# The setup phase of an attention kernel in another order

## The chip, the core and the metric

The kernel runs on one core of a Trainium2 chip. A core has a matrix engine (TensorE, PE in the profile, with its weight loads as PEld), a vector engine (VectorE, DVE), an activation engine (ScalarE, ACT), GpSimd (POOL) and SyncE (SP), which here only issues transfers. Each engine works through its own queue of instructions in order and waits on semaphores for the others. The metric is the device time of one execution in microseconds (us). A profile is a record of one such execution, and its times count from the start of its span.

## What is computed

With S = 2048 rows, D = 640 columns, 32 heads of 20 columns and F = 1728:

```python
xn = layernorm(x)                                  # rows of 640, eps 1e-5
q, k, v = split(xn @ wqkv)                         # 32 heads of 20
p = softmax(q @ k.T * 20 ** -0.5)                  # 2048 x 2048 for each head
s = (p @ v) @ wo
g = silu((sigmoid(xn @ w_gate) * (xn @ w_up)) @ w_down)
out = x + s * g
```

x, the weights and the result are bf16.

## The kernel before

**Tiling.** The 2048 rows lie in 16 tiles of 128 rows. The scores of one head for 512 queries and 128 keys fill one PSUM bank of 128 x 512. Four heads make a group; 4 query chunks times 8 groups give 32 passes of 64 banks, 2048 banks in all. The exponential of a bank is taken either on ACT (L868, two or three banks at a time, tiles `sc`) or on DVE with five instructions (L879 to L896, one bank at a time, tile `spare`).

**The main loop** is planned while the program is built. A planner keeps clocks of PE, ACT and DVE and emits, for PE, the next scores, the next products with V (L962, `oacc`), or a piece of a background job (tiles `work`, two PSUM banks): the rest of K (`k_job`: five matmuls of 128 x 512, an eviction L425 and a maximum L112 on DVE), the rest of V (`v_job`: five matmuls of 128 x 320 and a copy L129 on DVE), the queries of the next passes (`q_job`), the gate, up and down products, and the output. A job has a pass by which it must be done: V for the first 16 heads is due in pass 0, and so is K of group 1, without which the scores of pass 1 can't be computed. If such work is late, the planner emits it without scores between (`must_fill`). The engines then run the emitted order, at whatever pace the chip has.

**The setup phase** before it loads x in seven transfers and three weight blocks, computes the layernorm, and makes the first pass's operands: the transposed normalised rows `xnT`, K and its bound for group 0, Q for the first 512 queries and group 0, and V for the first 16 heads in 8 row tiles (`V_SETUP`). Its steps are listed as operations with an engine, an estimated duration, predecessors and a rank, and a list scheduler takes the one that can start first by these estimates; that gives the order of each engine's queue. The steps of a row tile t:

- `ln_stats` (DVE, L197 twice and L198): mean and variance
- `ln_sqrt` (ACT, L201) and `ln_scale` (DVE, L207 reciprocal, L208 product -mean/std), for one or two tiles at once
- `ln_apply` (L212): x * rstd + nb, on GpSimd for tiles 0 to 13, on DVE for 14 and 15
- `transpose` (PE, L220, five matmuls into a PSUM tile `tp`, three of them in turn) and `xnT_evict` (ACT, L223)

For four row tiles follow `k_mm` (PE, L102, PSUM tile `ps_k`, two in turn), `k_max` (DVE, L112) and `k_add` (ACT, L231); when all four are done, `k_bound` (DVE, L108 and L109, tile `bound`), `q_bound` (PE, L250, added into the query's PSUM bank) and `q_evict` (ACT, L255), which gives `qT`. The first scores need `qT`. The eight V products (PE, L124, tile `ps_v`) and their copies (ACT, L240) stand between.

GpSimd first clears and fills small tiles (L172 to L183), then applies the layernorm, pads the weights (`pad_copy`, L191), and after the list clears and fills what the main loop needs (L302 to L315), among it `wo_pad` (L311) and `identf`, behind which SP's 32 loads of `wo_pad` wait.

Of the kernel before, what the change touches and what calls it, by code (L numbers as in the profile page):

```python
# [8 lines left out]
FP32 = mybir.dt.float32  # L9
BF16 = mybir.dt.bfloat16  # L10
ACT = mybir.ActivationFunctionType
ALU = mybir.AluOpType
AXISX = mybir.AxisListType.X

P = 128
HEAD = 32
GH = 4
# [18 lines left out]
def kernel(  # L36
# [11 lines left out]
    nc = tc.nc  # L48
# [3 lines left out]
    S, D = x2.shape  # L52
    Dh = D // HEAD
    KD = D // P
# [52 lines left out]
    def k_bound(g):  # L107
        nc.vector.tensor_reduce(out=mk[:, g:g + 1], in_=mk_all[:, g, :], axis=AXISX, op=ALU.max)  # L108
        nc.vector.tensor_scalar(out=bound[:, g, :], in0=esum, scalar1=mk[:, g:g + 1], scalar2=None, op0=ALU.mult)  # L109

    def k_max(src, g, c):
        nc.vector.tensor_reduce(out=mk_all[:, g, c:c + 1], in_=src, axis=AXISX, op=ALU.max,  # L112
                                apply_absolute_value=True)

    def q_abs(ps):
        absq = wk.tile([P, QC], BF16, tag="absq", bufs=1, name="absq")
        high = ps.bitcast(U16).rearrange("p (q two) -> p q two", two=2)[:, :, 1]
        nc.vector.tensor_scalar(out=absq.bitcast(U16), in0=high, scalar1=0x7FFF, scalar2=None,
                                op0=ALU.bitwise_and)
        return absq  # L120
# [7 lines left out]
    def v_copy(copy, ps, tt, h0, h1):  # L128
        copy(out=v_all[:, tt, h0:h1, 1:1 + Dh],  # L129
             in_=ps[:, 0:(h1 - h0) * Dh].rearrange("p (h e) -> p h e", e=Dh))  # L130
# [8 lines left out]

    V_SETUP = 8
    qTs = {}
    with tc.tile_pool(name="setup", bufs=1) as sp, \
            tc.tile_pool(name="ps0", bufs=1, space=bass.MemoryType.PSUM) as ps0:
# [3 lines left out]
        stats = sp.tile([P, TT, 2, nc.vector.BN_STATS_DIM], FP32, name="stats")  # L149
        mv = sp.tile([P, TT, 2], FP32, name="mv")  # L150
        rstd = sp.tile([P, TT], FP32, name="rstd")
        nb = sp.tile([P, TT], FP32, name="nb")
        warm = sp.tile([P, 2], FP32, name="warm")

        def load_x(t0, n):
# [18 lines left out]
        nc.gpsimd.memset(v_all[:, :, 0:HH, 0:1], 1.0)  # L174
        make_identity(nc, ident)
        for w in (wkp, wqp):
            nc.gpsimd.memset(w[:, :, 0:GH, 0:1], 0.0)
            nc.gpsimd.memset(w[:, :, 0:GH, 1 + Dh:32], 0.0)
        nc.gpsimd.memset(e0, 0.0)
        nc.gpsimd.memset(esum, 0.0)  # L180
        for j in range(GH):
# [5 lines left out]
        def op(name, engine, took, after, fn, rank=0.0):  # L187
            ops.append((name, engine, took, after, fn, rank))

        def pad_copy(dst, raw, g0, g1):  # L190
            nc.gpsimd.tensor_copy(  # L191
                out=dst[:, :, GH * g0:GH * g1, 1:1 + Dh],
                in_=raw[:, :, GH * g0 * Dh:GH * g1 * Dh].rearrange("p k (h e) -> p k h e", e=Dh))

        def ln_stats(t):
            for i in range(2):
                nc.vector.bn_stats(out=stats[:, t, i, :], in_=x_sb[:, t, i * HALF:(i + 1) * HALF])  # L197
            nc.vector.bn_aggr(out=mv[:, t, :], in_=stats[:, t, :, :])  # L198

        def ln_sqrt(t0, n):  # L200
            nc.scalar.activation(out=rstd[:, t0:t0 + n], in_=mv[:, t0:t0 + n, 1], func=ACT.Sqrt,  # L201
                                 bias=eps_t, scale=1.0)
            if t0 + n == TT:
                nc.scalar.activation(out=warm[:, 1:2], in_=eps_t, func=ACT.Exp)

        def ln_scale(t0, n):
            nc.vector.reciprocal(out=rstd[:, t0:t0 + n], in_=rstd[:, t0:t0 + n])  # L207
            nc.vector.scalar_tensor_tensor(out=nb[:, t0:t0 + n], in0=mv[:, t0:t0 + n, 0], scalar=-1.0,  # L208
                                           in1=rstd[:, t0:t0 + n], op0=ALU.mult, op1=ALU.mult)

        def ln_apply(t, eng):
            eng.tensor_scalar(out=x_sb[:, t, :], in0=x_sb[:, t, :], scalar1=rstd[:, t:t + 1],  # L212
                              scalar2=nb[:, t:t + 1], op0=ALU.mult, op1=ALU.add)

        tps, kps, vps = {}, {}, {}

        def transpose(t):
            tps[t] = ps0.tile([P, KD, P], BF16, tag="tp", bufs=3, name="tp")
            for kd in range(KD):
                nc.tensor.transpose(out=tps[t][:, kd, :], in_=x_sb[:, t, kd * P:(kd + 1) * P], identity=ident)  # L220

        def xnT_evict(t):
            nc.scalar.activation(out=xnT[:, :, t * P:(t + 1) * P], in_=tps[t], func=ACT.Copy)  # L223

        def k_mm(c):
            kps[c] = ps0.tile([P, 512], FP32, tag="k", bufs=2, name="ps_k")
            for _ in k_matmuls(kps[c], 0, slice(c * 512, (c + 1) * 512)):
                pass

        def k_add(c):  # L230
            nc.scalar.activation(out=kT_all[:, 0, c * 512:(c + 1) * 512], in_=kps[c], func=ACT.Identity,  # L231
                                 bias=e0, scale=1.0)

        def v_mm(t):
            vps[t] = ps0.tile([P, 512], FP32, tag="v", bufs=2, name="ps_v")
            for _ in v_matmuls(vps[t], t, 0, HH):
                pass

        def v_evict(t):
            v_copy(lambda out, in_: nc.scalar.activation(out=out, in_=in_, func=ACT.Copy), vps[t], t, 0, HH)  # L240

        first = {}

# [11 lines left out]
            nc.scalar.activation(out=qT, in_=first["ps"], func=ACT.Copy, scale=q_scale)  # L255
            qTs[0, 0] = qT

        batches = [(0, 1), (1, 1), (2, 2), (4, 2), (6, 2), (8, 2), (10, 2), (12, 2), (14, 1), (15, 1)]
        for t in range(TT):
            op(("x", t), "SP", 0.0, [], None)  # L260
            ends["x", t] = 3.2 + 0.75 * t
            op(("stats", t), "DVE", 1.04, [("x", t)], lambda t=t: ln_stats(t), t * 0.01)
        for t0, n in batches:
            op(("sqrt", t0), "ACT", 0.29, [("stats", t0 + n - 1)], lambda t0=t0, n=n: ln_sqrt(t0, n), -1)
            op(("scale", t0), "DVE", 0.33, [("sqrt", t0)], lambda t0=t0, n=n: ln_scale(t0, n), -1)
            for t in range(t0, t0 + n):
                if t < TT - 2:
                    op(("apply", t), "POOL", 0.88, [("scale", t0)], lambda t=t: ln_apply(t, nc.gpsimd), -0.5)
                else:
                    op(("apply", t), "DVE", 0.4, [("scale", t0)], lambda t=t: ln_apply(t, nc.vector), -0.9)  # L270
                op(("tr", t), "PE", 0.7, [("apply", t)] + ([("xnT", t - 3)] if t > 2 else []),
                   lambda t=t: transpose(t), -0.5)
                op(("xnT", t), "ACT", 0.70, [("tr", t)], lambda t=t: xnT_evict(t), -0.5)
        op(("wkp",), "POOL", 0.52, [("x", 8)], lambda: pad_copy(wkp, wk_raw, 0, 1))
        op(("wqp",), "POOL", 0.52, [("x", 15)], lambda: pad_copy(wqp, wq_raw, 0, 1), 0.8)
        for c in range(4):
            op(("k", c), "PE", 1.2, [("xnT", 4 * c + i) for i in range(4)] + [("wkp",)]
               + ([("kmax", c - 2), ("kadd", c - 2)] if c > 1 else []), lambda c=c: k_mm(c))
            op(("kmax", c), "DVE", 0.69, [("k", c)], lambda c=c: k_max(kps[c], 0, c), 0.3 if c < 3 else -1)
            op(("kadd", c), "ACT", 0.48, [("k", c)], lambda c=c: k_add(c), 0.3 if c < 3 else -1)  # L280
        op(("kbound",), "DVE", 0.3, [("kmax", c) for c in range(4)], lambda: k_bound(0), -2)
        op(("q",), "PE", 1.2, [("xnT", t) for t in range(4)] + [("wqp",)], q_mm, 0.3)
        op(("qabs",), "DVE", 1.1, [("q",)], lambda: first.update(abs=q_abs(first["ps"])), 0.8)
        op(("qbound",), "PE", 0.3, [("qabs",), ("kbound",)], q_bound, -2)
        op(("qT",), "ACT", 0.48, [("qbound",), ("kadd", 3)], q_evict, -2)
        for t in range(V_SETUP):
            op(("v", t), "PE", 0.8, [("xnT", t), ("x", 15)] + ([("vd", t - 2)] if t > 1 else []),
               lambda t=t: v_mm(t), 0.9)
            op(("vd", t), "ACT", 0.44, [("v", t)], lambda t=t: v_evict(t), 0.9)

        free = {}
        waiting = [o for o in ops if o[4] is not None]
        while waiting:
            def start(o):
                return max([free.get(o[1], 0.0)] + [ends[a] + 0.12 for a in o[3]])
            ready = [o for o in waiting if all(a in ends for a in o[3])]
            o = min(ready, key=lambda o: start(o) + o[5])
            ends[o[0]] = free[o[1]] = start(o) + o[2]
            waiting.remove(o)
            o[4]()  # L300

        nc.gpsimd.memset(wkp[:, :, GH:HEAD, 0:1], 0.0)  # L302
        nc.gpsimd.memset(wkp[:, :, GH:HEAD, 1 + Dh:32], 0.0)
        pad_copy(wkp, wk_raw, 1, 2)
        nc.gpsimd.memset(wqp[:, :, GH:HEAD, 0:1], 0.0)
        nc.gpsimd.memset(wqp[:, :, GH:HEAD, 1 + Dh:32], 0.0)
        pad_copy(wqp, wq_raw, 1, 2)
        pad_copy(wkp, wk_raw, 2, NG)
# [802 lines left out]
```

## Time and profile before

| what | time |
| --- | --- |
| three runs | 983.74, 984.39 (median) and 987.81 us |
| the profiled execution | 984.3 us, of which the span is 982.3 us |
| first statistics (DVE L197) | 3.12 us |
| last normalised tile done (DVE L212) | 30.45 us |
| first scores (PE L846) | 47.54 us |
| first exponential (ACT L868) | 48.02 us |
| last exponential on ACT done | 955.10 us |
| share of the span that each engine is busy | PE 85%, DVE 89%, ACT 91%, POOL 25% |
| DVE in the setup: 32 of L197, 16 of L198 | 13.8 and 3.3 us |
| POOL in the setup: 14 of L212 | 12.1 us, 873 ns each |
| ACT in the setup: 16 of L223, 8 of L240 | 693 and 439 ns each |
| ACT, exponential of three banks, of two | 1537 and 1110 ns, x366 and x367 |

The time of a line in the timeline is its start and its length; "xN" merges N instructions that follow each other, and a bracket gives the idle time of the engine before it and who ended it. Instructions of one engine overlap a little in the records, so that the pace of a row is somewhat less than its mean length. In a table by windows, each engine has its busy time and the number of its instructions, and PEclk is the share of the full clock that TensorE was granted.

### The profile page before, as it was taken

The page shows a single profiled execution, that of the slowest core. Times are in us where ns is not written, and L with a number is a line of the kernel's source. Part 1 is how long each engine was busy: PE and PEld are TensorE (multiplying, and loading weights), DVE is VectorE, ACT ScalarE, POOL GpSimd, SP SyncE. Part 2 cuts the span into 40 slices and gives each one's busy share as a digit, 9 for nine tenths or more (in the row PEclk, how much of TensorE's full clock was granted, in tenths as well). Part 3 has the DMA queues.
Part 4 walks back from the last instruction along what each step waited for, and adds up shares of the span by engine and source line. Part 5 has one row for each costly group of instructions (what it writes and reads, how often), then busy time and mean ns, then how long its engine had stood idle before and what let it go on. Part 6 is the DMA issues. An engine that isn't in the chain of part 4 may idle for free.

```text
span 982.3 us, 16138 instructions
## 1 busy us (share of the span) xinstructions
PE 831.5 (85%) x5968; PEld 272.0 (28%) x5968; DVE 877.3 (89%) x1525; ACT 894.4 (91%) x848; POOL 243.6 (25%) x367
## 2 busy tenths in 40 slices
PE   4798888889989988988998888888988888989882
PEld 2332222222223322222331222222322222223321
DVE  7499999998889999889898989899998999799992
ACT  4598998999999999999998899999999899999970
POOL 6602021122211242222112332221122432201252
PEclk9799999999999999999997899999999899999985
DMA  5040000022211221322210212212120212210000
GB/s 207 22 130 12 3 13 12 12 47 66 66 39 47 75 66 54 71 57 49 59 63 26 57 48 53 53 46 46 43 62 35 66 46 57 61 42 13 12 25 27
DMA packets 92334, 48.84 MB, mean 50 GB/s; under 512 B 78724, under 2 KB 86820, under 8 KB 92256
## 3 DMA queue, kind: packets, MB, share of 16 engines
q1 hardware_dynamic: 83776, 33.03, 13.4%
q0 software_dynamic: 8480, 14.80, 4.8%
q8 instruction: 46, 0.75, 0.3%
q14 instruction: 32, 0.26, 0.1%
HBM read 40.74 MB, written 7.06 MB: 49 GB/s over the span
## 4 chain that ended last, share of the span: by engine, by line
DVE 37%; ACT 30%; PE 17%; issue 9%; POOL 0%; POOLq 0%; ACTq 0%; DVEq 0%
ACT p L868 28%; DVE du L892 7%; DVE du L889 6%; DVE de L879 6%; DVE p L896 6%; PE sc L846 6%; DVE dm L883 4%; PE oacc L962 3%; PE work L526 2%; PE work L504 2%; ACT tnh L498 2%; PE work L491 2%; DVE kT_all L425 1%; PE work L134 1%; DVE hT L508 1%
## 5 line engine op out<-in xcount | busy, mean ns | idle before, releaser
L868 ACT ACTIVATE p<-sc 128x1536 bf16<-128x1536 f32 (+1 forms) x733 | 849.4, 1323 | 32.2 <-PE sc L846 27.3
L846 PE MATMUL sc<-qT,kT_all 32*128 32x512 bf16 x1832 | 291.6, 391 | 70.6 <-ACT p L868 64.8
L879 DVE TENSOR_SCALAR de<-spare 128x512 int32<-128x512 f32 x216 | 147.6, 683 | 38.3 <-PE spare L846 36.5
L846 PEld LDWEIGHTS <-kT_all 32*128 32x128 bf16 x2048 | 86.6, 91 | 316.2 <-issue 305.9
L962 PE MATMUL oacc<-p,v_all 128*21 128x512 bf16 x2048 | 165.4, 393 | 2.9 <-DVE p L896 2.1
L896 DVE SCALAR_TENSOR_TENSOR p<-du,de 128x512 bf16<-128x512 f32 x216 | 156.8, 726 | 4.7
L892 DVE SCALAR_TENSOR_TENSOR du<-du,dm 128x512 f32<-128x512 f32 x216 | 156.8, 726 | 3.2
L889 DVE SCALAR_TENSOR_TENSOR du<-dm 128x512 f32<-128x512 f32 x216 | 154.3, 714 | 4.5
L633 POOL DMA_DIRECT2D den_dram<-oev x31 | 18.5, 597 | 353.8 <-DVE oev L632 353.8
L883 DVE TENSOR_SCALAR dm<-de 128x512 int32<-128x512 int32 x216 | 98.8, 457 | 0.9
L491 PE MATMUL work<-xnT,wg 128*128 128x512 bf16 (+1 forms) x280 | 84.3, 386 | 7.7 <-DVE de L879 6.1
L526 PE MATMUL work<-wd,hT 128*128 128x320 bf16 x448 | 89.4, 306 | 1.4 <-DVE d L530 0.5
L504 PE MATMUL work<-xnT,wu 128*128 128x512 bf16 (+1 forms) x280 | 81.6, 390 | 8.4 <-DVE de L879 7.5
L846 PE MATMUL spare<-qT,kT_all 32*128 32x512 bf16 x216 | 84.7, 392 | 1.4 <-DVE kT_all L425 0.6
L649 POOL DMA_DIRECT2D rl<-rec_dram x124 | 62.3, 508 | 52.6 <-DMA rec_dram<-den 49.5
L658 POOL TENSOR_TENSOR oT<-oev,rl 128x512 bf16<-128x512 f32 x31 | 43.0, 1386 | 57.7 <-DMA rl<-rec_dram 45.6
L962 PEld LDWEIGHTS <-v_all 128*21 128x21 bf16 x2048 | 30.5, 90 | 70.9 <-issue 69.8
L526 PEld LDWEIGHTS <-hT 128*128 128x128 bf16 x448 | 35.0, 98 | 52.7 <-issue 42.1
L134 PE MATMUL work<-xnT,wqp 128*128 128x512 bf16 x155 | 45.5, 387 | 3.0 <-DVE de L879 2.2
L581 PE MATMUL work<-wo_pad,oT 128*128 128x320 bf16 x192 | 39.3, 317 | 8.1 <-DVE de L879 5.7
L508 DVE SCALAR_TENSOR_TENSOR hT<-tnh,work 128x512 bf16<-128x512 bf16 (+1 forms) x56 | 38.0, 678 | 8.9 <-PE work L504 5.6
L643 POOL DMA_DIRECT2D rec_dram<-den x31 | 16.8, 543 | 113.0 <-DVE den L642 108.5
(100 smaller groups left out, 632.8 us busy)
## 6 DMA issues: line engine op xcount, KB each, us to landing
wg<-in_B_w_gate_dram SPq DMA_DIRECT2D x52, 160.0 KB
wu<-in_B_w_up_dram SPq DMA_DIRECT2D x52, 160.0 KB
rl<-rec_dram POOLq DMA_DIRECT2D x124, 64.0 KB, 2.3
gq_dram<-d POOLq DMA_DIRECT2D x12, 320.0 KB, 2.5
gqr<-gq_dram SPq DMA_DIRECT2D x12, 320.0 KB
xr<-in_A_x_dram SPq DMA_DIRECT2D x16, 160.0 KB
wd<-in_B_w_down_dram SPq DMA_DIRECT2D x1, 2080.0 KB
out_dram<-ot POOLq DMA_DIRECT2D x12, 160.0 KB, 2.6
```

Of the source, the lines that this page charges most:

```text
L491: nc.tensor.matmul(psg[0:fsz, :], lhsT=wg[:, kd, 0:fsz], rhs=xnT[:, kd, cols], start=(kd == 0), stop=(kd == KD - 1))
L504: nc.tensor.matmul(psu[0:fsz, :], lhsT=wu[:, kd, 0:fsz], rhs=xnT[:, kd, cols], start=(kd == 0), stop=(kd == KD - 1))
L526: nc.tensor.matmul(psd[:, 0:HALF], lhsT=hT[0:fsz, kf, t4 * P:(t4 + 1) * P], rhs=glu[1][0:fsz, kf, e0_:e1_], start=(kf == 0), stop=(kf == N ...
L649: nc.gpsimd.dma_start(out=t["rl"][32 * j:32 * j + 32, :], in_=rec_dram[n, j:j + 1, :].to_broadcast([32, QC]))
L846: nc.tensor.matmul(ps, lhsT=kT_all[32 * j:32 * j + 32, g, kt * P:(kt + 1) * P], rhs=qTs[qc, g][32 * j:32 * j + 32, :], start=True, stop=Tr ...
L868: nc.scalar.activation(out=buf.tile(), in_=ps, func=ACT.Exp, scale=exp_scale)
L879: nc.vector.tensor_scalar(out=t["e"], in0=ps, scalar1=BITS0, scalar2=-2.0 ** 31, op0=ALU.add, op1=ALU.max)
L883: nc.vector.tensor_scalar(out=t["m"], in0=t["e"], scalar1=0x7FFFFF, scalar2=0x3F800000, op0=ALU.bitwise_and, op1=ALU.bitwise_or)
L889: nc.vector.scalar_tensor_tensor(out=t["u"], in0=m, scalar=C2, in1=m, op0=ALU.add, op1=ALU.mult)
L892: nc.vector.scalar_tensor_tensor(out=t["u"], in0=t["u"], scalar=C1, in1=t["m"].bitcast(FP32), op0=ALU.add, op1=ALU.mult)
L896: nc.vector.scalar_tensor_tensor(out=buf.tile()[:, 0, :], in0=t["u"], scalar=C0, in1=t["e"].bitcast(FP32), op0=ALU.add, op1=ALU.mult)
L962: nc.tensor.matmul(oacc[32 * j:32 * j + 1 + Dh, :], lhsT=v_all[:, b % PER_PASS // GH, GH * g + j, 0:1 + Dh], rhs=buf.ap[:, i, :], start=(n ...
```

## The change

The setup phase gets another order and another split between the engines. Tiles 2 and 6 get their statistics on ACT (two passes over the tile with a summing output, one small instruction between); the product nb falls away, since normalising now subtracts the mean and then multiplies; all 16 tiles are normalised on GpSimd; tiles 2, 3, 6 and 7 get a square root and a reciprocal of their own. Three clears of padding (all of `wkp`, the first column of `wqp`) go to the front of DVE's queue; GpSimd's clears before and after the list shrink by them. PSUM has four turns of `tp` instead of three, three of `ps_k` instead of two, and none of its own for `ps_v`, which takes its turn among `tp`. Four V tiles are made in the setup instead of eight, copied by DVE (L129) and not by ACT; the other four become `v_job`s of the main loop, due in pass 0. The list scheduler gets new estimates, knows the turns of `tp`, and prefers, by a small weight, the operation with the longest chain behind it. The load of the exponential's table is an operation of its own.

```diff
-    V_SETUP = 8
+    V_SETUP = 4
...
         for w in (wkp, wqp):
-            nc.gpsimd.memset(w[:, :, 0:GH, 0:1], 0.0)
-            nc.gpsimd.memset(w[:, :, 0:GH, 1 + Dh:32], 0.0)
+            nc.vector.memset(w[:, :, :, 0:1], 0.0)
+        nc.vector.memset(wkp[:, :, :, 1 + Dh:32], 0.0)
+        nc.gpsimd.memset(wqp[:, :, 0:GH, 1 + Dh:32], 0.0)
...
+        ON_ACT = (2, 6)
...
+        def ln_sums(t):
+            nc.scalar.activation(out=junk, in_=x_sb[:, t, :], func=ACT.Identity, accum_out=sums[:, t:t + 1])
+            nc.scalar.activation(out=mv[:, t, 0:1], in_=sums[:, t:t + 1], func=ACT.Copy, scale=-1.0 / D)
+            nc.scalar.activation(out=junk, in_=x_sb[:, t, :], func=ACT.Square, bias=mv[:, t, 0:1],
+                                 accum_out=mv[:, t, 1:2])
+
         def ln_sqrt(t0, n):
             nc.scalar.activation(out=rstd[:, t0:t0 + n], in_=mv[:, t0:t0 + n, 1], func=ACT.Sqrt,
-                                 bias=eps_t, scale=1.0)
-            if t0 + n == TT:
-                nc.scalar.activation(out=warm[:, 1:2], in_=eps_t, func=ACT.Exp)
+                                 bias=eps_t, scale=1.0 / D if t0 in ON_ACT else 1.0)
 
         def ln_scale(t0, n):
             nc.vector.reciprocal(out=rstd[:, t0:t0 + n], in_=rstd[:, t0:t0 + n])
-            nc.vector.scalar_tensor_tensor(out=nb[:, t0:t0 + n], in0=mv[:, t0:t0 + n, 0], scalar=-1.0,
-                                           in1=rstd[:, t0:t0 + n], op0=ALU.mult, op1=ALU.mult)
-
-        def ln_apply(t, eng):
-            eng.tensor_scalar(out=x_sb[:, t, :], in0=x_sb[:, t, :], scalar1=rstd[:, t:t + 1],
-                              scalar2=nb[:, t:t + 1], op0=ALU.mult, op1=ALU.add)
+
+        def ln_apply(t):
+            nc.gpsimd.tensor_scalar(out=x_sb[:, t, :], in0=x_sb[:, t, :], scalar1=mv[:, t, 0:1],
+                                    scalar2=rstd[:, t:t + 1], op0=ALU.add if t in ON_ACT else ALU.subtract,
+                                    op1=ALU.mult)
...
+        KBUFS, TBUFS = 3, 4
...
         def v_mm(t):
-            vps[t] = ps0.tile([P, 512], FP32, tag="v", bufs=2, name="ps_v")
+            ps = ps0.tile([P, KD, P], BF16, tag="tp", bufs=TBUFS, name="ps_v")
+            vps[t] = ps.rearrange("p k d -> p (k d)").bitcast(FP32)
...
         def v_evict(t):
-            v_copy(lambda out, in_: nc.scalar.activation(out=out, in_=in_, func=ACT.Copy), vps[t], t, 0, HH)
+            v_copy(nc.vector.tensor_copy, vps[t], t, 0, HH)
...
-        batches = [(0, 1), (1, 1), (2, 2), (4, 2), (6, 2), (8, 2), (10, 2), (12, 2), (14, 1), (15, 1)]
+        batches = [(0, 1), (1, 1), (2, 1), (3, 1), (4, 2), (6, 1), (7, 1), (8, 2), (10, 2), (12, 2), (14, 1), (15, 1)]
...
+            if t in ON_ACT:
+                op(("stats", t), "ACT", 1.85, [("x", t)], lambda t=t: ln_sums(t))
+            else:
+                op(("stats", t), "DVE", 1.04, [("x", t)], lambda t=t: ln_stats(t))
...
-                if t < TT - 2:
-                    op(("apply", t), "POOL", 0.88, [("scale", t0)], lambda t=t: ln_apply(t, nc.gpsimd), -0.5)
-                else:
-                    op(("apply", t), "DVE", 0.4, [("scale", t0)], lambda t=t: ln_apply(t, nc.vector), -0.9)
...
+                op(("apply", t), "POOL", 0.86, [("scale", t0)], lambda t=t: ln_apply(t))
...
         for t in range(V_SETUP):
-            op(("v", t), "PE", 0.8, [("xnT", t), ("x", 15)] + ([("vd", t - 2)] if t > 1 else []),
-               lambda t=t: v_mm(t), 0.9)
-            op(("vd", t), "ACT", 0.44, [("v", t)], lambda t=t: v_evict(t), 0.9)
+            op(("v", t), "PE", 0.8, [("xnT", t), "wv"], lambda t=t: v_mm(t), 0.5)
+            op(("vd", t), "DVE", 0.4, [("v", t)], lambda t=t: v_evict(t), 0.5)
...
-            o = min(ready, key=lambda o: start(o) + o[5])
+            o = min(ready, key=lambda o: start(o) + o[5] - 0.001 * below[o[0]])
...
-        nc.gpsimd.memset(wkp[:, :, GH:HEAD, 0:1], 0.0)
-        nc.gpsimd.memset(wkp[:, :, GH:HEAD, 1 + Dh:32], 0.0)
         pad_copy(wkp, wk_raw, 1, 2)
-        nc.gpsimd.memset(wqp[:, :, GH:HEAD, 0:1], 0.0)
         nc.gpsimd.memset(wqp[:, :, GH:HEAD, 1 + Dh:32], 0.0)
```

In the order that is built, GpSimd's queue after its first clears is: tiles 0 to 3, the first copy of `wkp`, tiles 4 to 9, the first copy of `wqp`, tiles 10 to 15, then a copy of `wkp`, the clear of `wqp`, a copy of `wqp`, the two large copies, the clears of `v_all` and `wo_pad`, `identf` and `pick`. On PE the last part of the setup is: K of chunk 1, the transposes of tiles 12 to 15, K of chunks 2 and 3, V of tiles 0 and 1, the bound, V of tiles 2 and 3, the first scores. On DVE the reciprocal of tile 15 stands behind the first `k_max`, and `bound` ahead of the four copies of V.

In the main loop DVE takes 215 banks instead of 216. At the end of pass 0, 34 matmuls stand on PE between two groups of scores (28 of K, five of Q, one for the bound); before, they were 14 with eight products with V. At the end of pass 3 they are 17 of K, Q and the bound, before 14. Every other stretch between two groups of scores holds eight matmuls of such jobs or fewer, besides products with V, in both orders.

## The prediction

> **What bounds the kernel now.** I read the span first (982.3 us; the run took 984.3, so 2.0 lie around it; the median of the runs, 984.39, is the same within 0.1). Then the setup's timeline, then the windows behind it.
>
> ```profile
> 25.35 0.52 POOL L191 COPY wqp<-wq_raw 128x400 bf16<-128x400 bf16 x1
> 25.44 2.53 DVE L212 TENSOR_SCALAR x_sb<-x_sb,rstd,nb 128x640 bf16<-128x640 bf16 x1
> 25.80 0.71 POOL L302 MEMSET wkp<- 128x140 bf16 x1
> 26.10 1.70 POOL L303 MEMSET wkp<- 128x1540 bf16 x1
> ...
> 35.84 4.67 POOL L311 MEMSET wo_pad<- 128x5120 bf16 x1
> ...
> 38.85 1.86 DVE L109 TENSOR_SCALAR bound<-esum,mk 128x128 bf16<-128x128 bf16 x1
> ...
> 40.77 0.53 PE L250 MATMUL ps_q<-absq,bound 128*128 128x512 bf16 x1 [2.68 <-DVE bound L109]
> ...
> 41.09 6.51 PE L124 MATMUL ps_v<-wv,xnT 128*128 128x320 bf16 x35
> ...
> 47.54 0.39 PE L846 MATMUL sc<-qT,kT_all 32*128 32x512 bf16 x3
> ```
>
> Up to 30.45 the setup waits for the statistics on DVE: two tiles take 2.75 (L197 starts at 17.98 and 20.73), with a wait for ACT's root in each pair. Afterwards it waits for K, for `bound`, and for seven V tiles that stand on PE ahead of the first scores. DVE's L212 is held from 25.44 until GpSimd's copy and both clears are over (27.80), and L109, whose mean elsewhere is 0.25 (eight of mean 0.455, so (8 x 0.455 - 1.86)/7), until the clear of `wo_pad` ends at 40.51.
>
> ```profile
> core 0: us, PE busy (x) PEld busy (x) DVE busy (x) ACT busy (x) POOL busy (x), PEclk, DMA share, GB/s
> 60.00:70.00 10.00, 8.68 (x63) 2.87 (x61) 9.90 (x18) 10.00 (x10) 0.00 (x0) 1.00 0.37 92
> 70.00:80.00 10.00, 7.98 (x56) 2.63 (x59) 9.28 (x19) 4.99 (x5) 0.00 (x0) 1.00 0.01 2
> 80.00:90.00 10.00, 9.09 (x65) 2.62 (x64) 9.96 (x21) 10.00 (x10) 1.85 (x3) 1.00 0.01 2
> ...
> 78.09 6.89 ACT L868 ACTIVATE p<-sc 128x1536 bf16<-128x1536 f32 x6 [5.01 <-PE sc L846]
> ...
> 162.03 19.10 ACT L868 ACTIVATE p<-sc 128x1024 bf16<-128x1024 f32 x17 [4.07 <-PE sc L846]
> ```
>
> In the main loop ACT is full with exponentials and DVE nearly so. ACT starves twice for long, 5.01 and 4.07 us, where the K and Q of the next pass are late. Nothing later makes such a loss good, since ACT has no other slack.
>
> **The change part by part.** I carry the new queues forward by rows.
>
> *Statistics and normalising.* DVE keeps 14 tiles at 1.04 (L197 starts 6.63 and 7.67), 14.6; twelve reciprocals at 0.15 and one L112 ahead of the last, 2.4. From 3.12 that gives 20.1 without waits. GpSimd does four tiles, waits for wk_raw until 10.3 (its copy started at 10.32 before), then 12 tiles at 0.87 and two copies at 0.52: 21.8. Two waits push this: the statistics of tiles 2 and 6 on ACT delay its first evictions to about 9.9, so that the root of tile 15 queues behind them, and the first L112 stands ahead of the last reciprocal. My pass through the queues ends the last tile at 23.4, not 30.45. Bounds: 21.8 and 25.5. No row shows a summing activation; I take 1.85 for both passes and the small one, between two L223 and one L201 (1.6) and three L223 and one L201 (2.4), which moves the end by -0.4 and +1.0. The tiles' DMAs are issued as before.
>
> *Clears on DVE.* 2080 elements; GpSimd's rate, 1.70 for 1540, makes 2.3 from 0.75, done at 3.1: hidden under the wait for the first tile (3.12). If they are held like L212 until GpSimd's first clears end (about 3.3), they end at 5.6, and the pass moves by 1.5 to 2. I take zero.
>
> *From the last tile to `bound`.* The third turn of `ps_k` ends the 1.38 that chunk 2's K waited for L112 before 32.80; the exponential's table (1.28 + 0.20) loads under K, with no other ACT work due; V's turns of `tp` are free when the last L223 ends (27.5). PE still has transposes and K of chunks 2 and 3 to do. At the slow rows (2.2 for K at 20.24, 0.7 for a tile) K ends at 31.3, and with L112 (0.69) and L108 (0.2) `bound` is ready to run at 32.4. At the fast rows (0.45 for a tile at 19.10, K at half) it is 28.6. The Trainium skill says that TensorE goes to full clock after some 3.4 us of sustained work (TensorE: Matmul & The Clock Gate, "Part 1: The HAM clock gate"); here 4.4 us of unbroken work from 32.80 stayed at a granted 0.50. The next step makes the difference nearly void.
>
> *`bound` again under a clear.* GpSimd's queue after its last tile holds, by pace, 0.55 + 1.70 + 0.55 + 2.13 + 2.12 + 0.82 + 4.67 = 12.5 up to the end of `wo_pad`, whose clear runs from 31.3 to 36.0. `bound` comes between 28.6 and 32.4: under the last copy, or a clear. The row at 25.44 was not let in where the copy gave way to a clear, nor between clears, so I hold it to 36.0 and end it at 36.2. The Trainium skill has the loser of the port that DVE and GpSimd share wait for the whole instruction (SBUF — State Buffer, "SBUF: two separate sides"). By that alone `bound` under the copy would run at 30.5, and the sum below would be 5.6 lower.
>
> *V.* Only two tiles follow the bound, at 0.68 (last L240 spacing) to 1.33 (42.67 to 44.00) each. From 36.3 with 0.3 for L250 and 2.1 for two: first scores at 38.7, against 47.54. **Setup: -8.8**, bounds -6.5 and -14.4. The copies on DVE come behind `bound` and hold up nobody. The first exponential also waits for GpSimd's large copies, done at 30.5. SP's 32 loads of wo_pad come behind `identf`, some 4 us earlier, and the weights behind them too; nobody waits.
>
> *Four V jobs in pass 0.* PE gets 4 x 0.68, DVE 4 x 0.41, and K of group 1 is pushed back to the end of the pass: 34 matmuls in one block without scores. Before, 71.46 to 77.59 took 6.1. After, by paces of DVE in that stretch: first K product 0.9; five L425 at 0.66, four L112 at 0.59, L883 0.33, L889 0.60, L118 0.60, L108 0.17, L109 0.25, together 7.6; from there to scores 1.2 (76.38 to 77.59), 0.4 for a PSUM bank, 0.3 for the scores in front: 10.4. **+4.3**, bounds +2 (part of it would have been lost anyway) and +7 (each bank waited for). The second block has three more K: 0.65 on PE, up to 2 with DVE; **+0.8**. One exponential grows from two banks to three: 1537 - 1110 = **+0.4**. DVE has one bank fewer and four copies more, off the path.
>
> Sum: -8.8 + 4.3 + 0.8 + 0.4 = -3.3. 982.3 - 3.3 = 979.0, with 2.0 around it 981.0.
>
> **The rivals.** *`bound` slips in early.* If it gets the port at the end of a copy (30.5), scores come at 33.1: 5.6 less, 975.4. For it: the product L208 at 12.07 lasted 0.49 and ended at 12.56, between two tiles of GpSimd, so some ends do let DVE in. Against: the two ends at 25.87 and 26.51 did not. 0.19.
>
> *The V jobs cost nothing net.* If ACT idles as long at the end of pass 0 as before, the loss is 1.2 and the time 976.7. For it: DVE takes eight banks in pass 0 rather than seven, and PE is busy only 8.7 of 10. Against: those 34 matmuls alone are 7.3 on PE. 0.13.
>
> *The clears on DVE are held.* Setup -6.9, time 982.9. For: the row at 25.44. Against: L389, a clear by DVE, took 0.48 with GpSimd clearing beside it, though it clears PSUM. 0.10.
>
> *The starving recurs (the slower side).* V, K and Q fall behind in pass 0 and stay due pass by pass: each end of passes 1 to 4 starves ACT as at 162.03, 4.1 a time. One more such loss brings 985.1, level with before; from the second on the kernel is slower (989.2), with three 993.3. For: DVE is 98% busy from 60 to 180, so late work stays late. Against: only two long blocks stand in the new order, at the same two places. 0.11.
>
> That it does not do what it says can be left out: the queues show the order.
>
> **How the numbers follow.** The forecast has 0.47, with 978.5 to 983.5 as its own range. Half a per cent, about what a measurement of this kernel tells from no change, is 4.9: faster means below 979.5, slower above 989.3. Faster: 0.47 x 0.28 + 0.19 x 0.9 + 0.13 x 0.85 = 0.41. Slower: most of the last rival, 0.09. Same: 0.50. The range goes from 974.5, where `bound` is early, to 986.5, where the setup gains 6.5 and the blocks cost 9; one tenth lies beyond each end.
>
> **What would show it.** The last L218 (was L212) ends near 23.4 on GpSimd; L109 is long (over 1.5) and ends with the clear of `wo_pad` near 36; first scores near 38.7; one idle time of ACT of 9 near the end of pass 0 (some 72 to 80) and one of 5 at the end of pass 3; no other above 2. The forecast is wrong if L109 is short, if the V jobs leave ACT's first long idle at 5, if DVE's first statistics start after 4, or if ACT idles 4 us at further ends of passes.

## The result, and the profile after

The changed kernel takes 1000.03 us, the median of four runs (997.56 to 1002.93), against 985.88 of four runs of the kernel before: a ratio of 1.0145, with a 95% interval from 1.0107 to 1.0183. It is slower, by about 14 us. The profiled execution (a run of 997.56) has a span of 995.5 us.

The timeline of the changed kernel's setup, from the last tiles to the first exponential:

```profile
28.82 14.89 POOL L218 TENSOR_SCALAR x_sb<-x_sb,mv,rstd 128x640 bf16<-128x640 bf16 x6
...
48.03 2.18 POOL L193 COPY wqp<-wq_raw 128x2400 bf16<-128x2400 bf16 x1
...
48.74 7.09 DVE L109 TENSOR_SCALAR bound<-esum,mk 128x128 bf16<-128x128 bf16 x1
...
50.16 1.21 POOL L329 MEMSET v_all<- 128x256 bf16 x1
50.96 4.67 POOL L330 MEMSET wo_pad<- 128x5120 bf16 x1
...
55.89 0.61 PE L259 MATMUL ps_q<-absq,bound 128*128 128x512 bf16 x1 [6.83 <-DVE v_all L129]
...
56.29 2.88 PE L124 MATMUL ps_v<-wv,xnT 128*128 128x320 bf16 x10
...
59.75 0.61 PE L865 MATMUL sc<-qT,kT_all 32*128 32x512 bf16 x3 [0.59 <-DVE v_all L129]
...
60.46 1.45 ACT L887 ACTIVATE p<-sc 128x1536 bf16<-128x1536 f32 x1 [3.33 <-DMA wo_pad<-in_A_wo_dram]
```

The first line is the result: six tiles take 14.89 us on GpSimd, 2.48 each, where a tile took 873 ns before. The last tile is done at 43.71, where the forecast had 23.4. In the kernel before, the last one was done by DVE, at 30.45:

```profile
29.76 0.69 DVE L212 TENSOR_SCALAR x_sb<-x_sb,rstd,nb 128x640 bf16<-128x640 bf16 x1
```

What follows looks as forecast, only later: `bound` (L109) asks at 48.74 during a copy, is let in neither where the copy gives way to a clear (50.16) nor between clears (50.96), and ends at 55.83 with the clear of `wo_pad`. Two brackets name something else than the cause. PE's product at 55.89 needs `bound`; the copies of V that its bracket names stand behind `bound` on DVE and end at the same time. The first exponential starts 0.1 after its scores end (59.75 + 0.61), and in the run with `bound` on ACT further down it starts before the loads of `wo_pad` do, so it doesn't need the load that its bracket names.

The view of the tile `x_sb` gives shortest, median and longest duration in ns of GpSimd's normalising, and two lines of the timeline show where the short ones are:

```profile
L218 POOL TENSOR_SCALAR x_sb<-x_sb,mv,rstd x16: 864/2488/2507, 6.3 to 41.2; 128x640 bf16<-128x640 bf16 x16
```

```profile
11.29 0.87 POOL L218 TENSOR_SCALAR x_sb<-x_sb,mv,rstd 128x640 bf16<-128x640 bf16 x1
12.15 2.49 POOL L218 TENSOR_SCALAR x_sb<-x_sb,mv,rstd 128x640 bf16<-128x640 bf16 x1
```

Same line, same shape, same engine, back to back, and a factor of 2.9 between them. The short one is tile 6. Its mean comes from ACT with its sign turned, so that it is normalised by (add, mult), as is tile 2. The other fourteen go by (subtract, mult).

The windows around the end of pass 0, and the two long idle times of ACT, which answer to those at 78.09 and 162.03 before:

```profile
core 0: us, PE busy (x) PEld busy (x) DVE busy (x) ACT busy (x) POOL busy (x), PEclk, DMA share, GB/s
72.00:82.00 10.00, 9.04 (x74) 3.22 (x73) 9.79 (x20) 9.95 (x10) 0.00 (x0) 1.00 0.70 207
82.00:92.00 10.00, 8.61 (x48) 3.25 (x48) 9.93 (x18) 4.99 (x5) 0.00 (x0) 1.00 0.00 0
92.00:102.00 10.00, 8.33 (x54) 2.58 (x52) 9.48 (x18) 5.50 (x5) 0.79 (x1) 1.00 0.01 2
```

```profile
96.50 20.46 ACT L887 ACTIVATE p<-sc 128x1536 bf16<-128x1536 f32 x18 [9.45 <-PE sc L865]
...
180.90 20.65 ACT L887 ACTIVATE p<-sc 128x1024 bf16<-128x1024 f32 x18 [4.95 <-PE sc L865]
```

ACT stands still for 9.45 and 4.95 where it stood still for 5.01 and 4.07, at the same two places and nowhere else for over 2 us after the first exponential's own wait.

The span falls into three stages: up to the first exponential on ACT, from there to the end of the last one on ACT (main), and the rest (tail). Each row is one profiled execution.

| kernel | last tile normalised | first scores | first exponential | main | tail | span |
| --- | --- | --- | --- | --- | --- | --- |
| before | 30.45 | 47.54 | 48.02 | 907.1 | 27.2 | 982.3 |
| after | 43.71 | 59.75 | 60.46 | 909.2 | 25.9 | 995.5 |

So the setup loses 12.4, the main loop 2.1, and the tail gives 1.3 back: +13.2. The loss is the setup's.

### The profile page after: what moved, and what is told of

Same layout as the page of the kernel before. It is cut to its first block, busy times and chain, and to the rows that moved or that the text cites. A ratio compares the mean times of both kernels' runs of the same rounds, so it can differ in the third digit from the quotient of the medians.

```text
span 995.5 us, 16117 instructions
## 1 busy us (share of the span) xinstructions
PE 831.4 (84%) x5968; PEld 273.0 (27%) x5968; DVE 880.8 (88%) x1515; ACT 895.8 (90%) x852; POOL 266.1 (27%) x363
## 4 chain that ended last, share of the span: by engine, by line
DVE 34%; ACT 33%; PE 15%; issue 12%; POOL 4%; DMA 1%; SPq 1%; POOLq 0%; ACTq 0%; DVEq 0%
ACT p L887 31%; DVE du L908 6%; DVE de L898 6%; DVE du L911 5%; DVE p L915 5%; PE sc L865 5%; DVE dm L902 3%; PE oacc L981 2%; POOL x_sb L218 2%; ACT tnh L517 2%; PE work L523 1%; PE work L545 1%; PE work L510 1%; DVE kT_all L444 1%; PE work L102 1%
## 5 line engine op out<-in xcount | busy, mean ns | idle before, releaser
L887 ACT ACTIVATE p<-sc 128x1536 bf16<-128x1536 f32 x733 | 849.8, 1321 | 37.2 <-PE sc L865 28.3
L908 DVE SCALAR_TENSOR_TENSOR du<-dm 128x512 f32<-128x512 f32 x215 | 155.2, 722 | 5.3
L915 DVE SCALAR_TENSOR_TENSOR p<-du,de 128x512 bf16<-128x512 f32 x215 | 154.3, 718 | 4.7
L545 PEld LDWEIGHTS <-hT 128*128 128x128 bf16 x448 | 35.2, 98 | 51.7 <-issue 41.9
L102 PE MATMUL work<-xnT,wkp 128*128 128x512 bf16 x140 | 39.7, 381 | 8.3 <-DVE kT_all L444 3.5
```

Source lines behind the costliest of these rows:

```text
L545: nc.tensor.matmul(psd[:, 0:HALF], lhsT=hT[0:fsz, kf, t4 * P:(t4 + 1) * P], rhs=glu[1][0:fsz, kf, e0_:e1_], start=(kf == 0), stop=(kf == N ...
L887: nc.scalar.activation(out=buf.tile(), in_=ps, func=ACT.Exp, scale=exp_scale)
L908: nc.vector.scalar_tensor_tensor(out=t["u"], in0=m, scalar=C2, in1=m, op0=ALU.add, op1=ALU.mult)
L915: nc.vector.scalar_tensor_tensor(out=buf.tile()[:, 0, :], in0=t["u"], scalar=C0, in1=t["e"].bitcast(FP32), op0=ALU.add, op1=ALU.mult)
```

## The experiments

All ratios are to runs of the kernel before on the same chip, with their 95% interval. Those runs have medians from 982.73 to 985.88, so that two kernels which ran beside different ones are best compared by their ratios; where both readings are given, the difference of the medians stands first. The first three ask whether the pair of operations alone makes the price; the next four what holding `bound` costs; the last three what the V tiles cost.

**Pairs of operations, priced alone.** Before the list, the kernel before gets eleven GpSimd instructions on one 128 x 640 tile, with the same two scalars and nothing else to wait for:

```diff
+        for a, c in PAIRS:
+            if c is None:
+                nc.gpsimd.tensor_scalar(out=jout, in0=jin, scalar1=eps_t, scalar2=None, op0=a)
+            else:
+                nc.gpsimd.tensor_scalar(out=jout, in0=jin, scalar1=eps_t, scalar2=eps_t, op0=a, op1=c)
```

> The kernel before, with eleven extra GpSimd tensor_scalar instructions on a spare 128 x 640 bf16 tile ahead of the first normalised tile, one for each pair of operations, all with the same scalar. If the operation sets the price (theory): every one with subtract takes about 2.5 us, mult and add in either order about 0.87. If the new surroundings set it (rival: scalars just written by other engines, a port shared with DVE): all pairs take 0.87. The setup is longer by the sum of the eleven, some 10 to 20 us; this is a look at prices, not at the total.

The pairs stand in this order: (mult, add), (add, mult), (subtract, mult), (mult, subtract), (subtract, add), (add, add), (mult, mult), (max, mult); then mult, add and subtract alone. GpSimd's timeline:

```profile
4.72 0.88 POOL L195 TENSOR_SCALAR jout<-jin,eps_t 128x640 bf16<-128x640 bf16 x1
5.70 0.87 POOL L195 TENSOR_SCALAR jout<-jin,eps_t 128x640 bf16<-128x640 bf16 x1
6.67 2.51 POOL L195 TENSOR_SCALAR jout<-jin,eps_t 128x640 bf16<-128x640 bf16 x1
...
14.50 2.50 POOL L195 TENSOR_SCALAR jout<-jin,eps_t 128x640 bf16<-128x640 bf16 x1
17.10 0.88 POOL L195 TENSOR_SCALAR jout<-jin,eps_t 128x640 bf16<-128x640 bf16 x1
18.08 2.50 POOL L195 TENSOR_SCALAR jout<-jin,eps_t 128x640 bf16<-128x640 bf16 x1
...
20.68 1.89 POOL L193 TENSOR_SCALAR jout<-jin,eps_t 128x640 bf16<-128x640 bf16 x1
```

(mult, add), (add, mult) and (mult, mult) take 0.87 to 0.88; every other pair 2.50 or 2.51, (add, add) among them; and one operation alone, mult too, 1.89. So it is not that a subtraction is dear: three pairs are cheap and all else tried is not, even less work. Of these eleven the change took a cheap one away and put a dear one in its place. The kernel's own time (1001.24, one run) is of no interest, since eleven instructions stand ahead of its setup.

**The kernel before, with the subtraction.** Its normalising on GpSimd, tiles 0 to 13, gets the pair of the change; nothing else differs:

```diff
+            if eng is nc.gpsimd:
+                eng.tensor_scalar(out=x_sb[:, t, :], in0=x_sb[:, t, :], scalar1=mv[:, t, 0:1],
+                                  scalar2=rstd[:, t:t + 1], op0=ALU.subtract, op1=ALU.mult)
+                return
```

> The kernel before, with one edit: the 14 tiles on GpSimd are normalised by subtract and mult (mean, std) instead of mult and add. Theory (subtract costs 2.49 against 0.87): 14 x 1.62 = 22.7 us more on GpSimd, of which DVE's pace hides about half: the last tile on GpSimd ends near 41 instead of 25.4, and the first scores come about 10 us later, near 57; total about +10 us. Rival (the surroundings of the changed kernel made it slow): 0.87 a tile, no change from the kernel before.

The view of the tile `x_sb`:

```profile
L213 POOL TENSOR_SCALAR x_sb<-x_sb,mv,rstd x14: 2488/2492/2557, 5.0 to 38.3; 128x640 bf16<-128x640 bf16 x14
```

All fourteen are slow, in the old order and with the old split. The first exponential comes at 63.15, 15.1 later than before, and the one run took 999.67 beside 984.06. The expectation had some 10: `bound` asks at 50.20 instead of 38.85, 11.4 later, and is then held for 5.88 instead of 1.86, which makes up the rest. The pair alone makes a loss of the result's size; nothing of the new order is needed for it.

**The change, with an addition.** The mean of the other fourteen tiles gets its sign turned in one small DVE instruction for each `ln_scale`, and all tiles use (add, mult):

```diff
+            if t0 not in ON_ACT:
+                nc.vector.tensor_scalar(out=mv[:, t0:t0 + n, 0], in0=mv[:, t0:t0 + n, 0], scalar1=-1.0,
+                                        scalar2=None, op0=ALU.mult)
...
-                                    scalar2=rstd[:, t:t + 1], op0=ALU.add if t in ON_ACT else ALU.subtract,
+                                    scalar2=rstd[:, t:t + 1], op0=ALU.add,
```

> The changed kernel, with the mean negated by twelve small DVE instructions so that all 16 tiles use add and mult on GpSimd. Theory (the price of subtract was the one step that failed): 0.87 a tile, the last tile ends at 24 to 25, the bound is still held until wo_pad is clear, first scores near 39.5, ACT idle 9 at the end of pass 0 and 5 at the end of pass 3, total 980 to 983, about 0.995 to 0.998 of before. Rival A (surroundings): tiles stay at 2.3, total 998 or more. Rival B (the main loop lost more than the two long idle times): tiles at 0.87 but total 986 or more.

983.70 us over ten runs, ratio 0.9997 [0.9976, 1.0019]: 16.3 us less than the change (14.6 by the ratios), and level with the kernel before. The timeline:

```profile
19.38 3.44 POOL L221 TENSOR_SCALAR x_sb<-x_sb,mv,rstd 128x640 bf16<-128x640 bf16 x4 [0.38 <-DVE mv L217]
...
26.51 8.43 DVE L109 TENSOR_SCALAR bound<-esum,mk 128x128 bf16<-128x128 bf16 x1
...
30.06 4.68 POOL L333 MEMSET wo_pad<- 128x5120 bf16 x1
...
35.40 2.87 PE L124 MATMUL ps_v<-wv,xnT 128*128 128x320 bf16 x10
...
38.86 0.61 PE L868 MATMUL sc<-qT,kT_all 32*128 32x512 bf16 x3 [0.59 <-DVE v_all L129]
...
39.57 1.45 ACT L890 ACTIVATE p<-sc 128x1536 bf16<-128x1536 f32 x1 [3.33 <-DMA wo_pad<-in_A_wo_dram]
```

Four tiles in 3.44; the last is done at 22.82 (forecast 23.4) and the first scores come at 38.86 (forecast 38.7). This is the setup that the prediction described. Yet the first exponential is 8.4 us earlier than before (39.57 against 48.02) and the time is the same. `bound` is held for 8.43 us here, and afterwards something takes 8 us back; the next four runs look into both. The main stage has grown by 12.8 in the profiled executions (919.9 against 907.1; the profiled run of the change with an addition was one of its longer ones, 987.43).

**`bound` of group 0 on ACT.** Its product is an activation with a scale:

```diff
+        if g == 0:
+            nc.scalar.activation(out=bound[:, g, :], in_=esum, func=ACT.Copy, scale=mk[:, g:g + 1])
+            return
```

With the addition:

> As the run with add everywhere, and the bound of group 0 made by ACT instead of DVE, so that it shares no port with GpSimd. Theory (the bound is held by GpSimd's clears and sets the first scores): the bound takes 0.3, first scores 3 to 6 us earlier than in the run with add alone, total 975 to 979. Rival (the first scores wait for something else, the V tiles or GpSimd's copies under the tiles of the main loop): the same as with add alone, within 1 us.

```profile
27.08 0.39 ACT L110 ACTIVATE bound<-esum,mk 128x128 bf16<-128x128 bf16 x1
...
27.52 0.39 PE L265 MATMUL ps_q<-absq,bound 128*128 128x512 bf16 x1 [0.34 <-ACT bound L110]
...
27.75 1.52 PE L127 MATMUL ps_v<-wv,xnT 128*128 128x320 bf16 x10
...
28.63 0.49 DVE L132 CAST v_all<-ps_v 128x320 bf16<-128x320 f32 x1 [0.92 <-PE ps_v L127]
...
29.86 0.39 PE L871 MATMUL sc<-qT,kT_all 32*128 32x512 bf16 x3 [0.59 <-DVE v_all L132]
...
30.39 4.69 POOL L336 MEMSET wo_pad<- 128x5120 bf16 x1
...
33.47 2.04 DVE L908 TENSOR_SCALAR dm<-de 128x512 int32<-128x512 int32 x1
```

The product takes 0.39 us and the first scores come at 29.86, 9.0 earlier, more than the 3 to 6 expected. The time is 969.26, ratio 0.9861 [0.9813, 0.9910]: 14.4 less than with `bound` held (13.4 by the ratios), though the first exponential is only 9.2 earlier. The same two V tiles take 1.52 on PE here and 2.87 there, so the hold has a second price: TensorE comes out of it at half its clock (granted 1.00 from 26.5 to 29.9 here, 0.50 from 34.9 to 38.8 there). The clear of `wo_pad` still holds something, at a lower price: the main loop now starts beside it, and L908, which takes 0.42 at 38.95, takes 2.04 here. PE then waits 1.72 for DVE, and ACT 1.38 for the next scores.

The same edit alone on the change, where the subtraction stays:

> The changed kernel as it is, with subtract on GpSimd, and only the bound moved to ACT. Theory (two separate faults, the price of subtract some 20 us of setup, the held bound some 9 us): first scores 9 us earlier than in the changed kernel (near 51), granted clock 1.0 at the start of the main loop, total 986 to 990. Rival (with the slow tiles GpSimd's clears come so late that the bound costs nothing of its own): within 2 us of the changed kernel.

993.74 us, ratio 1.0119 [1.0072, 1.0165], above the 986 to 990 expected. Against the change that is 6.3 less by the medians and 2.6 by the ratios, whose intervals overlap; the profiled spans differ by 7.3 (988.2 and 995.5), nearly all of it the first exponential, 7.5 earlier (53.01). The size stays loose, but with the hold gone the kernel is still slower than before: the hold is not the cause of the loss.

And on the kernel before:

> The kernel before with one edit, the bound of group 0 made by ACT. Its hold behind the clear of wo_pad lasted 38.85 to 40.71. Theory: the bound takes 0.4 and ends near 39.2, PE stays warm (it was at half clock from 41 to 44), so first scores come 1.5 to 4 us earlier, near 44 to 46, total 980 to 983. Rival (in the kernel before, the V tiles set the first scores whatever the bound does): first scores move by less than 1 us, total unchanged.

982.76 over nine runs, ratio 0.9969 [0.9943, 0.9996]: 1.1 less by the medians and 3.0 by the ratio. The first exponential comes 3.1 earlier (44.95 against 48.02), with PE granted 1.00 from 41 to 44, where it had 0.50. There the hold was 1.86 us only.

**The clock after the hold.** The hold stays, but PE is given 30 matmuls into a bank that nobody reads, queued ahead of the product with `bound`, so that it works while it would wait:

```diff
+            for i in range(30):
+                nc.tensor.matmul(kps[1], lhsT=ident, rhs=xnT[:, 0, 0:512], start=True, stop=True,
+                                 skip_group_check=True)
```

> The run with add everywhere, and 30 matmuls of 128 x 512 with no use on PE ahead of the bound's product, while PE waits for the held bound; they write a K bank that is done with. The hold stays. Theory (the hold also lets TensorE's clock fall, and the main loop starts at half clock for some 8 us): first scores near 37.5 instead of 38.9, granted clock 1.0 in the first 8 us of scores instead of 0.5, total 2 to 6 us below add alone. Rival (the clock does not matter there, ACT sets the pace): first scores 1.3 us earlier at most, total the same within 1.5 us.

`bound` is held as long as without the 30 matmuls (8.44 us from 26.80), but the two V tiles behind it take 1.52 instead of 2.87. Windows after the hold, first of the change with an addition, then with the 30 matmuls:

```profile
core 0: us, PE busy (x) PEld busy (x) DVE busy (x) ACT busy (x) POOL busy (x), PEclk, DMA share, GB/s
38.00:42.00 4.00, 3.41 (x15) 1.18 (x14) 1.47 (x3) 1.96 (x2) 0.00 (x0) 0.50 0.25 69
42.00:46.00 4.00, 4.00 (x19) 1.07 (x17) 2.52 (x5) 2.88 (x3) 0.00 (x0) 0.50 0.26 70
46.00:50.00 4.00, 4.00 (x31) 1.41 (x27) 3.44 (x7) 3.23 (x3) 0.00 (x0) 0.80 0.63 141
```

```profile
core 0: us, PE busy (x) PEld busy (x) DVE busy (x) ACT busy (x) POOL busy (x), PEclk, DMA share, GB/s
38.00:42.00 4.00, 3.70 (x30) 1.80 (x27) 2.31 (x6) 3.88 (x4) 0.00 (x0) 1.00 0.29 66
42.00:46.00 4.00, 3.90 (x32) 1.51 (x29) 3.93 (x8) 4.00 (x4) 0.00 (x0) 1.00 0.28 71
```

From 38 to 46 PE has 15 and 19 matmuls at a granted 0.50 where it has 30 and 32 at 1.00, and ACT is busy 4.84 of 8 us where it is busy 7.88. The kernel takes 977.29 over ten runs, ratio 0.9937 [0.9911, 0.9962]: 6.4 us less (5.9 by the ratios), of which 1.45 is the earlier first exponential (38.12). The other 4.5 to 5 come after it, and main is 5.3 shorter in the profiles (914.6 against 919.9): the price of the low clock.

How long the low clock lasts differs from kernel to kernel, each seen in one execution. It is granted in full again 12.7 us after the end of the hold with the addition (near 47.6) and 7.7 after it in the change (63.5), but 3.4 after it with eight V tiles in the setup (38.8, the next run) and 3.6 in the kernel before (44.3). The first two have PE stand still for 0.59 in front of the first scores, while the clock is still low; the other two don't. Whether that pause is what prolongs it was not tried.

**Eight V tiles in the setup again.** One number is changed back:

```diff
-    V_SETUP = 4
+    V_SETUP = 8
```

With `bound` held:

> The run with add everywhere, and eight V tiles in the setup again instead of four. PE's order in the main loop is then that of the kernel before, with 14 matmuls at the end of pass 0 instead of 34. Theory (the four V jobs cost 4 to 5 us in the main loop and save 4 x 0.68 to 1.33 in the setup): first scores 3 to 5 us later than with add alone (42 to 44), ACT idle 5 and 4 at the two ends instead of 9.4 and 4.9, total within 2 us of add alone. Rival (the V jobs are free, since PE and DVE have room): 3 to 5 us slower than add alone. Rival (they cost more): faster by over 3 us.

977.88, ratio 0.9948 [0.9930, 0.9966]. The first exponential is 3.0 later than with four tiles (42.57), and the time 5.8 less (4.8 by the ratios). But here the clock is back before the first scores (from 42 to 50 it is granted at 1.00), so this run alone doesn't price the V tiles.

With `bound` on ACT, where the clock is at 1.00 either way:

> Add everywhere, the bound on ACT, and eight V tiles in the setup. Theory: PE is warm, so four more V tiles cost 4 x 0.68 = 2.7 us before the first scores (near 32.6 instead of 29.9), and the idle times of ACT at the two ends fall by 4.4 and 0.9; net 2 to 3 us faster than with four V tiles, 966 to 968. Rival (V jobs are free in the main loop): 2.7 slower, 972.

970.48, ratio 0.9878 [0.9841, 0.9916], against 969.26 with four tiles. The profiled executions show three terms: four tiles bring the first exponential 2.6 earlier (30.34 against 32.94), cost 4.0 in main (910.7 against 906.7), and gain 2.5 in the tail (26.1 against 28.6). The tail's term is in the windows, with four tiles and then with eight:

```profile
core 0: us, PE busy (x) PEld busy (x) DVE busy (x) ACT busy (x) POOL busy (x), PEclk, DMA share, GB/s
942.00:948.00 6.00, 4.22 (x30) 2.82 (x30) 2.69 (x7) 0.00 (x0) 1.56 (x2) 0.96 0.00 0
```

```profile
core 0: us, PE busy (x) PEld busy (x) DVE busy (x) ACT busy (x) POOL busy (x), PEclk, DMA share, GB/s
942.00:948.00 6.00, 5.19 (x22) 4.34 (x23) 1.52 (x4) 0.00 (x0) 0.18 (x1) 0.50 0.00 0
```

The output's products at the end run at 0.96 of the clock in the one and at 0.50 in the other. Why the clock falls there with eight tiles was not tried. Nor are the 4.0 in main all the price of the V jobs: with four tiles the main loop meets the clear of `wo_pad` (L908, 2.04 above), with eight it starts later and doesn't (0.42 at 36.07). In sum four tiles and eight can't be told apart; the gain of 2 to 3 us that was expected from eight did not come.

Six tiles, the number between:

> Add everywhere, the bound on ACT, six V tiles in the setup: between the runs with four and with eight. Its order has 26 matmuls at the end of pass 0 without scores (34 with four, 14 with eight). If the cost of V jobs is linear: first scores 31.2, ACT idle about 7 at the end of pass 0, total within 1.5 us of the other two (968 to 971). If the block costs only above some size, it is the best of the three, by 1 to 2 us.

967.46, ratio 0.9841 [0.9807, 0.9876], with one long idle time of 7.75. Its median is the lowest of the kernels run, but its interval overlaps those with four and eight, so that the choice among them stays open. What these three share is the addition and `bound` on ACT.

## Why the prediction was wrong

**The step that failed** is "12 tiles at 0.87" in "Statistics and normalising". 0.87 is the row of another pair, (mult, add); the change's pair (subtract, mult) takes 2.49 in the same place. The prediction carried it from one pair to the other on the strength of engine, shape and type, and gave it no bound, although the trace of before had no row of that pair. Its bounds of 21.8 and 25.5 for the last tile moved only the waits around the price. Fourteen tiles at 2.49 - 0.87 are 22.7 us; the first exponential moved by 20.9 (60.46 against 39.57), and the time by 14.6 to 16.3. The rest, 4.6 to 6.3, came back after the first exponential. In the profiled executions the main stage is 10.7 longer with the addition, which overstates it, since they are the fastest run of the change and one of the longest with the addition. They show where it went: with the addition `bound` is held for 8.43 and the first 8 us of the main stage have a granted 0.50, in the change 7.09 and 0.81. None of the rivals had it: the slower one was about the main loop, which did not starve.

**With the pair corrected, the setup's sum holds.** Last tile 22.82 for 23.4, first scores 38.86 for 38.7, but two of its parts were off and cancelled:

- `bound` asked at 26.51, earlier than the forecast's bounds of 28.6 to 32.4. From 20 to 26.5 PE was granted 1.00, and the last two K took 2.32 together, not 2.2 each.
- `bound` ended at 34.94 with the clear of `wo_pad`, as forecast by the held row (36.2 there; GpSimd's queue after its last tile took 11.9, not 12.5, and the last tile ended earlier). From there the forecast had 2.5 to the first scores, with 2.1 for two V tiles, between the spacing of V at full clock (0.68 each) and at half (1.33). It took 3.9 at a granted 0.50, with 2.87 for the two V tiles and then 0.59 in which the scores wait for DVE's last copy of V. The prediction said of these copies that they "hold up nobody"; the same 0.59 stands in front of the first scores in the change.

The choice between row and rule was right. The rule read from the Trainium skill (SBUF — State Buffer, "SBUF: two separate sides"), that the loser waits for the whole instruction, would have let `bound` in at the end of the copy. In three kernels here (25.44 before, 48.74 after, 26.51 with the addition) DVE was held across several GpSimd instructions and let in at the end of a long clear (27.80, 55.63, 34.74), although GpSimd had more to do next. Why these ends let it in and the others didn't stays open.

**What the forecast left out: the clock after the hold.** It said that the hold made the question of the clock "nearly void". It is the other way round: the hold is what lets the clock fall. That is some 5 us of the main stage, shown by the 30 matmuls, and more than the 2.7 by which the change with an addition, at 983.70, lies above the forecast of 981.0. The Trainium skill's figure of some 3.4 us of sustained work until full clock (TensorE: Matmul & The Clock Gate, "Part 1: The HAM clock gate") would by itself bring the clock back at about 38.3, as an estimate from 34.9 on. The run with eight V tiles and the kernel before agree with that figure (3.4 and 3.6 us). The change with an addition does not: PE was busy 10.42 of 11.1 us from 34.9 to 46 and was granted 0.50 throughout, and 0.80 from there to 50.

**Four V jobs in pass 0: the idle times right, the loss too large.** Forecast 9 and 5 us of idle ACT, measured 9.45 and 4.95 (9.41 and 4.85 with the addition). The +4.3, +0.8 and +0.4 were summed as a loss of 5.5; the change's main and tail together lost 0.8 (+2.1 and -1.3). ACT is idle for 36.8 us of the whole main stage, before for 35.2: the two long idle times grew by 5.3, and all others together shrank by 3.8, so ACT did have slack elsewhere, against "since ACT has no other slack". In the pair with `bound` on ACT the loss in main is 4.0, not all of it the V jobs', and 1.5 net of the tail.

**Clears on DVE: 0.9, not zero.** DVE's timeline at the start:

```profile
2.58 1.52 DVE L179 MEMSET wkp<- 128x1760 bf16 x1 [0.29 <-issue]
4.02 0.82 DVE L201 BATCH_NORM_STATS2 stats<-x_sb 128x6 f32<-128x320 bf16 x2
```

The first statistics start at 4.02, not 3.12, by a hair one of the prediction's own signs of being wrong (after 4). There are gaps of 0.51 and 0.29 between the clears, and the long one takes 1.52 and ends at 4.10. No run has it without GpSimd beside it, so it is not shown whether a hold is part of this. The rival that had the clears held until 5.6 fell. Little hung on it: with the addition the last tile still ended 0.6 ahead of its forecast.

**Sums on ACT: 1.85 forecast, 1.92 measured** (5.58 to 7.50 in the changed kernel). The view of `x_sb` shows an instruction that the estimate by eviction rows couldn't have:

```profile
L205 ACT ACTIVATE junk<-x_sb x2: 722/729/736, 5.6 to 8.1; 128x640 bf16<-128x640 bf16 x2
L205 ACT ACTIVATION_READ_ACCUMULATOR junk<-x_sb x2: 186/186/187, 6.2 to 8.7; 128x1 f32 x2
```

Each summing output is read by an instruction of its own, 0.19 us.

**The rivals.** `bound` did not slip in early. The V jobs came near to costing nothing in the changed kernel, by other means than that rival had: not by an unchanged first idle time, but by less idle time elsewhere and a shorter tail. The starving did not recur.

## What to carry to other kernels

A price belongs to an operation with its operands, not to an engine and a shape: when a change swaps the pair of operations in an instruction that stands many times on the path, the row of the old pair is one bound and not the price (here the two were a factor of 2.9 apart). A short instruction that is held behind another engine's long ones costs the hold and can then cost a slow clock on TensorE, if that waited for it; giving it to an engine that isn't held (0.39 us on ACT here) was worth some 14 us in the kernel with the addition. Where an earlier stage ends 8 us sooner and the time stays, look at the clock of the first microseconds after it.

## What the runs showed of the hardware

- GpSimd's two-operation form on 128 x 640 bf16 takes 0.87 to 0.88 for (mult, add), (add, mult) and (mult, mult), 2.49 to 2.51 for the five other pairs tried, and 1.89 for a single mult, add or subtract. Why was not found out.
- DVE's product of 128 x 128 in SBUF waited up to 8.43 us across GpSimd copies and clears, while DVE's copies from PSUM ran beside them (0.49 at 28.63, with `bound` on ACT, under a copy of 2.19 that started at 27.46), and ACT's product too (0.39 at 27.08).
- After PE had done 0.34 us of work in 8.4 (26.5 to 34.9, with the addition), the granted clock stayed at 0.50 for at least 11 us of nearly full work (34.9 to 46). After holds in other kernels it was back sooner: 7.7 us in the change, 3.6 in the kernel before, 3.4 with eight V tiles.
